# Two sweeps walked backwards with three blocks kept in SBUF, and 1/den and a gradient turned by DMA, in a four-layer forward and backward kernel

## The chip, the cores and the metric

The kernel runs on one core of a Trainium2 chip, as one launch. Its metric is the device time of that launch in microseconds (us). The engines are called by the profile's names: PE is TensorE (its matmuls), PEld TensorE's weight loads, DVE VectorE, ACT ScalarE, POOL GpSimd and SP SyncE, which here only issues DMAs.

## The reference

x has S = 2048 tokens of D = 512. Four layers follow each other, a linear attention A (layers 0 and 2) and a gated layer B with F = 1376 (layers 1 and 3), with the same weights in both pairs:

```python
def A(x, wqkv, wo):                      # H = 32 heads of 16
    q, k, v = heads(x @ wqkv)
    pq, pk = phi(q), phi(k)              # phi(t) = where(t > 0, t + 1, exp(t)) + 1e-6
    kv = einsum("bhsd,bhse->bhde", pk, v)
    z = einsum("bhsd->bhd", pk)
    num = einsum("bhqd,bhde->bhqe", pq, kv)
    den = einsum("bhqd,bhd->bhq", pq, z)[..., None] + 1e-6
    return merge(num / den) @ wo
def B(x, w_gate, w_up, w_down):
    return (sigmoid(x @ w_gate) * (x @ w_up)) @ w_down
x = x + A(layernorm(x));  x = x + B(layernorm(x))      # layers 0 and 1
x = x + A(layernorm(x));  x = x + B(layernorm(x))      # layers 2 and 3
```

The outputs are the last x and the gradients, for a given grad_out, of the input x and of wqkv, wo, w_gate, w_up and w_down. The layernorm has no weights.

## The kernel before, in words

*Tiles and sweeps.* The tokens are cut into 8 blocks of 256 (NBLK, TB). kv and z need every token of a layer before the first q can be used, and the backward pass has the same barrier, so the work is done in five sweeps over the blocks, with a small stage at each barrier, and a last stage for the weight gradients:

- sweep1 (L1492): layernorm of layer 0, k and q of layer 0 (a_k L581, a_q L766), then the barrier (a_barrier L679).
- sweep2 (L1521): the second half of attention layer 0 (a_p2 L796), layer 1 forward (glu_fwd L1188), layernorm and k of layer 2, and its barrier. q of blocks 0 and 1 reuses the turned activations that k used (hTk, kept); for the others h is loaded and turned again (hTq, L773).
- sweep3 (L1550): the second half of attention layer 2 (a_p2), layer 3 forward and backward in one (glu_both L1274), first half of the backward of layer 2 (a_b1 L882), and its barrier (a_bbarrier L983).
- sweep4 (L1589): the second half of the backward of layer 2 (a_b2 L1085), backward of layer 1 (glu_bwd L1383), a_b1 of layer 0, and its barrier.
- sweep5 (L1618): a_b2 of layer 0.
- dw (L1640): weight gradients, the matmuls of L1716, whose operands (dw_set) are loaded and turned by DMA.

All five sweeps take the blocks in the order 0 to 7. What one sweep hands to the next goes through DRAM: x as f32 (xf_d, 512 KB a block, stores SX, loads LX in sweep3), the gradient of x as f32 (dxa_d and dxb_d, 512 KB a block, stores SDX, loads LDX), h, pk, pnT, rphi, dqT and dkT in bf16 (256 KB a block), and layer 1's hh, s2t, and du and dg pairs.

*1/den, in a_p2.* den (DE) is a product of PE with 32 columns of heads per 128 tokens; VectorE adds EPS, takes the reciprocal and writes it as two bf16 parts, high and rest (rr). turn (RT) turns these by two PE transposes (rT_ps). spread (SP) then spreads each head over its 16 rows: four matmuls of 256 columns per block with a matrix of ones and zeros put r_ps in PSUM. VectorE multiplies pq by it (L844, pnT), makes phi' from pq (L847) and multiplies that by r_ps as well (L849, rphiT). pnT is needed by ya_ps (L856), the projection of the attention's output, and pnT and rphi are stored for a_b1.

*The gradient, in a_b1.* ACT casts the gradient of x to bf16 (g), and add_turn (L484) turns it by eight PE transposes a block (L479, gT_ps) and two ACT copies out of PSUM (L481). gT feeds dpn_ps (L914).

*Weights turned for the backward pass.* load_w11T (L1478) loads wdT, wuT and wgT by DMA transposes, the last two in two DMAs each (L1486, L1487). As 1376 is not a multiple of 128, the first rows of the last piece are set to zero by a memset on POOL; load_w11 (L1463) does the same for wd. wgT is then scaled by -0.5 on VectorE.

*What sets the order.* Every step is a piece given to the planner (class Plan, L75): G.add for a step with PE work and the steps of other engines behind it (post, with an engine letter and a duration), G.load and G.store for DMAs. The planner walks through a model of the time before the program is built: a piece may start when its dependencies are met and its buffers (TOKENS, L297: among them 5 PSUM tiles mm, 2 accumulators acc, 20 tiles t2 of 256 KB, 5 tiles xb of 512 KB, 6 tiles s1, 3 pairs pr) are free, and among those that can start on an engine the one with the highest priority goes. The priority is the length of the chain behind a piece, plus a hand-set number from the table OFFSETS (L284). A DMA costs its megabytes by RATE (L87). Each engine executes in the order that comes out. All DMAs are issued on SP's queue, in one order: one whose data is not ready holds those behind it.

The lines of the spread, which the change replaces for six blocks of each attention layer:

```python
for c2 in range(2):
    nc.tensor.matmul(ps[:, c2, :], lhsT=k.spread[:, 2 * hf + c2, :], rhs=st["rT"][:], start=True, stop=True)
yield
sl = slice(2 * hf, 2 * hf + 2)
nc.vector.tensor_tensor(A.pn[b][:, sl, :], pq[:, sl, :], ps[:], ALU.mult)
yield
ph = s1(k, "phq")
nc.vector.tensor_scalar(ph[:], flat(pq[:, sl, :]), -EPS, 1.0, ALU.add, ALU.min)
yield
nc.vector.tensor_tensor(flat(A.rphi[b][:, sl, :]), ph[:], flat(ps[:]), ALU.mult)
```

Of the kernel before, what the change touches and what calls it, by code (L numbers as in the profile page):

```python
# [74 lines left out]
class Plan:  # L75
# [11 lines left out]
    RATE = 0.27  # L87
# [17 lines left out]
    def load(self, key, fn, mb, deps=(), use="", pull=0.0):  # L105
        self.add(key, fn, 0.0, deps, [("D", mb / self.RATE)], use, pull=pull)

# [172 lines left out]
ACCJ, ACCY = 11, 7  # L280
SUMS = {1: ([0, 1], -1), 3: ([2, 3], 1), 5: ([4, 5], 3), 6: ([6], 5), 7: ([7], 6)}
# [3 lines left out]
    CB1:1=-7 DE0:1=-63,2=-19,4=+5,7=+5 DE2:1=-23 DK0:2=+1,4=+21 DP0:0=+36,1=-28,2=+36,3=+36,5=-102 DP2:2=+63,6=-51  # L285
    DT0:+83 DW1:0=-30 DW3:1=+1,7=-2 E3:0=-31,1=+2 G11:0=-7,6=+24,7=+66 G3:1=+1 GS0:3=+31,5=-1,6=-86 GS2:5=+7,6=+44
    J0:1=-74 K0:3=-12 K2:0=+28,1=+28,2=+28,3=+28,4=+29,6=+44,7=+10 LB2:1=-93 LB3:2=-52,3=-12,6=+63,7=+106 LDH0:0=-49
    LDH2:3=+97 LDL0:0=+53,2=+38 LDP0:1=-6 LDP2:3=+41 LDQ0:3=+67 LDX0:0=+113 LDX2:1=-102,2=-13 LG3:0=+7 LH1:6=-75
    LN0:1=-131,5=-68,6=+58 LN2:0=-1 LP0:7=-44 LS1:1=-57 MS0:5=-40 MS2:1=-12,5=-34,7=-87
    Q0:1=-103,2=-115,4=-101,5=-22 Q2:0=-1,1=-23,2=+8 RT0:2=+7 RT2:2=+47 S0:+44 S2:-3 SG2:-64 SH1:2=+17 SN0:4=+50  # L290
    SP0:0=-66 SP2:1=-6,5=-11,7=+1 SPREAD:-24 SQ2:0=+2,6=-77 SU1:3=+1,6=-21 SV1:0=-15,3=+22,6=-13
    TG0:0=+6,1=+3,2=+7,4=+3,5=-18 TG2:6=+38 TK0:2=+113,5=+22,6=+48 TK2:7=+55 TR1:3=-11 UT0:2=-98,3=+2 WGT:-26
    WPL0:+56 WT0:0=-35,1=-40 Y33:7=-97 YA2:5=-43 ZE0:0=+1,3=-2 ZE2:2=+16,4=+19,6=+151 ZS0:5=-8,7=+136 ZS2:7=-52
    ZZ0:+35
# [7 lines left out]
def kernel(  # L302
# [38 lines left out]
    k.rphi_d = {l: dt_(f"rphi_d{l}", [D, S]) for l in (0, 2)}  # L341
# [21 lines left out]
    for l in (0, 2):  # L363
        for nm in ("hT", "pk", "pq", "pn", "rphi", "bh"):
            setattr(k.A[l], nm, {})
# [132 lines left out]
def load_turn(k, key, src, put, name, deps, pull=0.0):  # L498

    def ld():  # L500
        t = t2(k, name)
        put(t)
        k.nc.sync.dma_start_transpose(out=t[:], in_=src)
    k.G.load(f"{key}.0", ld, BLK, deps, "+t2", pull)
    k.G.add(f"{key}.1", lambda: None, 0.0, [f"{key}.0"])


def layernorm(k, l, b, x_fn, deps, sums=False):

    nc, G = k.nc, k.G  # L510

    def half_sums(j):
# [3 lines left out]
        col = slice(2 * b + j, 2 * b + j + 1)  # L516
        rs, sx = k.rstd[l][:, col], k.sx[l][:, col]
# [18 lines left out]
    def half(j):  # L536
# [3 lines left out]
        col = slice(2 * b + j, 2 * b + j + 1)  # L540
# [24 lines left out]
    G.store(f"SH{l}.{b}", lambda: nc.sync.dma_start(out=tok3(k.h_d[l], b), in_=k.h[l, b][:]), BLK, [f"LN{l}.{b}.{j}@h" for j in range(2)])  # L565
# [15 lines left out]
def a_k(k, l, b, keep, by_dma=False):  # L581
# [3 lines left out]
    n = f"{l}.{b}"  # L585

# [9 lines left out]
    if by_dma:  # L596
        load_turn(k, f"TK{n}", k.h_d[l][brows(b), :], put, "hTk", [f"SH{n}"])
    else:
        add_turn(k, f"TK{n}", lambda: k.h[l, b], put, "hTk", [[f"LN{n}.{j}@h"] for j in range(2)])
# [5 lines left out]
    G.store(f"SPK{n}", lambda: nc.sync.dma_start(out=tok3(k.pk_d[l], b), in_=A.pk[b][:]), BLK, [f"K{n}.{j}" for j in range(2)])  # L605
# [160 lines left out]
def a_q(k, l, b, keep, deps):  # L766
    nc, G = k.nc, k.G
    A = k.A[l]
    n = f"{l}.{b}"

    def ld():
        A.hT[b] = t2(k, "hTq")
        nc.sync.dma_start_transpose(out=A.hT[b][:], in_=k.h_d[l][brows(b), :])  # L773

    def half(hf):
# [3 lines left out]
        for c2 in range(2):  # L779
            for m in range(NDC):  # L780
                nc.tensor.matmul(ps[:, c2, :], lhsT=k.wq[:, m, cslice(2 * hf + c2)], rhs=A.hT[b][:, m, :],  # L781
                                 start=(m == 0), stop=(m == NDC - 1))
        yield
        yield from phi(k, flat(A.pq[b][:, 2 * hf:2 * hf + 2, :]), flat(ps[:]))
    if keep:
        src = [f"TK{n}.0", f"TK{n}.1"]
    else:
        G.load(f"LQ{n}", ld, BLK, [f"SH{n}", f"<K{n}.1"] + deps, "+t2")
        src = [f"LQ{n}"]
# [3 lines left out]
    G.free("-t2", [f"<Q{n}.1", f"<K{n}.1"])  # L793


def a_p2(k, l, b, xin_fn, deps, late):  # L796
# [4 lines left out]
    n = f"{l}.{b}"  # L801

# [3 lines left out]
    def den():  # L806
# [9 lines left out]
        yield  # L816
        r = k.p1.tile([P, 2, H], F32, name="rcp", tag="rcp", bufs=2)
# [8 lines left out]
    def turn():  # L826
# [5 lines left out]
        nc.vector.tensor_copy(st["rT"][:], flat(tps[:]))  # L832

# [17 lines left out]
    def y(j):  # L851
# [3 lines left out]
        for c in range(NDC):  # L855
# [4 lines left out]
    G.load("LX" + n, lx, BLK if l == 0 else 2 * BLK, [f"YA{l}.{b - 2}.1", f"SX{l - 1}.{b}"] + deps, "+t2" if l == 0 else "+xb")  # L860
    G.add("DE" + n, den, 8 * 0.027, [f"Q{n}.0", f"Q{n}.1", f"ZZ{l}", f"<YA{l}.{b - 2}.1"],
          [("V", 0.22, "+dn -tp"), ("V", 0.55), ("V", 0.2, "+rr"), ("V", 0.22, "-dn")], "+tp")
    G.add("RT" + n, turn, 2 * C128, ["DE" + n, "SPREAD"] + late, [("V", 0.29, "-tp +rT")], "+tp -rr")
    for hf in range(2):
        G.add(f"SP{n}.{hf}", lambda hf=hf: spread(hf), 2 * C256, ["RT" + n] + ([f"<SP{n}.0"] if hf else []),
              [("V", 0.68, "@pn"), ("V", 0.29, "+s1"), ("V", 0.68, "-s1 -mm")], "+mm" if hf else "+mm +t2 +t2")
    pn = [f"SP{n}.{hf}@pn" for hf in range(2)]
    G.free("-rT", [f"<SP{n}.1"])
    G.free("-t2", [f"SP{n}.0", f"SP{n}.1"])
    G.store(f"SN{n}", lambda: nc.sync.dma_start(out=dmaj(k.pnT_d[l], b), in_=A.pn[b][:]), BLK, pn)  # L870
    G.store(f"SR{n}", lambda: nc.sync.dma_start(out=dmaj(k.rphi_d[l], b), in_=A.rphi[b][:]), BLK, [f"SP{n}.{hf}" for hf in range(2)], "-t2")
# [10 lines left out]
def a_b1(k, l, b, deps):  # L882

    nc, G = k.nc, k.G
# [6 lines left out]
    def ld():  # L891
        A.pn[b] = t2(k, "pnTl")
        nc.sync.dma_start(out=A.pn[b][:], in_=dmaj(k.pnT_d[l], b))
        A.rphi[b] = t2(k, "rphiTl")
        nc.sync.dma_start(out=A.rphi[b][:], in_=dmaj(k.rphi_d[l], b))

    def ldt():
        st["pn"] = t2(k, "pn", [P, 2, D])
        nc.sync.dma_start_transpose(out=st["pn"][:], in_=k.pnT_d[l][:, brows(b)])
# [7 lines left out]
    def dpn(hf):  # L907
# [3 lines left out]
        for c2 in range(2):  # L911
            c = 2 * hf + c2
            for m in range(NDC):
                nc.tensor.matmul(ps[:, c2, :], lhsT=A.WpT[:, m, cslice(c)], rhs=st["gT"][:, m, :],  # L914
# [24 lines left out]
    G.load("LN_" + n, ldt, BLK, [f"SN{n}", f"<MS{l}.{b - 2 if b % 2 else b - 3}.3", f"<DP{l}.{b - 2}.0"] + deps, "+t2")  # L939
# [3 lines left out]
    add_turn(k, f"TG{n}", lambda: st["g"], lambda t: st.__setitem__("gT", t), f"gT{l}", [[f"CA{n}.{j}"] for j in range(2)], pull)  # L943
# [8 lines left out]
    G.store(f"SQ{n}", lambda: nc.sync.dma_start(out=dmaj(k.dqT_d[l], b), in_=st["dq"][:]), BLK, [f"ZE{n}.{hf}" for hf in range(2)], "-t2")  # L952
    if b in MSUMS:
# [26 lines left out]
        G.free(" ".join(["-t2"] * 2 * len(bs)), [f"<MS{n}.3"] + [f"<TG{l}.{bb}.1" for bb in bs])  # L980
# [77 lines left out]
def ln_bwd(k, l, b, j, dh_ps, h, x_in, x_out):  # L1058

    nc = k.nc  # L1060
    rs = (k.rstdh if l in k.rstdh else k.rstd)[l][:, 2 * b + j:2 * b + j + 1]
# [15 lines left out]
def add_lnb(k, l, b, fn, deps, ps_tag, more=""):  # L1077

    for j in range(2):
        k.G.add(f"LB{l}.{b}.{j}", lambda j=j: ln_bwd(k, l, b, j, *fn(j)), 0.0, deps[j] + ([f"LB{l}.{b}.0@s"] if j else []),  # L1080
# [4 lines left out]
def a_b2(k, l, b, x_load, out, deps, out_use=""):  # L1085
# [4 lines left out]
    n = f"{l}.{b}"  # L1090

# [3 lines left out]
    def ldt(nm, src):  # L1095
        st[nm] = t2(k, nm)
        nc.sync.dma_start_transpose(out=st[nm][:], in_=src[brows(b), :])

    def ldq():
        st["dqT"] = t2(k, "dqTl")  # L1100
        nc.sync.dma_start(out=st["dqT"][:], in_=dmaj(k.dqT_d[l], b))

    def ldh():
        st["h"] = t2(k, "hl", [P, 2, D])
        nc.sync.dma_start(out=st["h"][:], in_=tok3(k.h_d[l], b))
# [26 lines left out]
    G.load("LDH" + n, lambda: ldt("hT", k.h_d[l]), BLK, pre, "+t2")  # L1132
    G.load("LDP" + n, lambda: ldt("pkT", k.pk_d[l]), BLK, pre, "+t2")
    G.load("LDQ" + n, ldq, BLK, pre + [f"SQ{n}"], "+t2")
    G.load("LDL" + n, ldh, BLK, pre, "+t2")
    G.load("LDX" + n, ldx, 2 * BLK, pre + [f"SDX{l + 1}.{b}"], "+xb")
# [4 lines left out]
    G.store(f"SK{n}", lambda: nc.sync.dma_start(out=dmaj(k.dkT_d[l], b), in_=st["dkT"][:]), BLK, [f"DK{n}.{hf}" for hf in range(2)])  # L1141
# [3 lines left out]
    add_lnb(k, l, b, lambda j: (st["ps", j][:], st["h"][:, j, :], st["x"][:, j, :], out(st["x"], j)),  # L1145
            [[f"DH{n}.{j}", "LDL" + n, "LDX" + n] for j in range(2)], "mm", out_use)
    G.free("-t2 -t2", [f"<DH{n}.1"])
# [40 lines left out]
def glu_fwd(k, l, b):  # L1188
# [3 lines left out]
    n = f"{l}.{b}"  # L1192
    x = k.x
# [35 lines left out]
    for p in range(NPAIR):  # L1229
# [5 lines left out]
        G.add(f"Y{n}.{p}", lambda p=p: y(p), q * 2 * C512, [f"G{n}.{p}@hh", "WD"] + ([f"<Y{n}.{p - 1}"] if p else []),  # L1235
              [("V", 0.77, "-acc @0"), ("V", 0.77, "-acc")] if p == NPAIR - 1 else [], "" if p else "+acc +acc")
    G.free("-t2", [f"<G{n}.5"])
    G.store("SHH" + n, lambda: store_hh(k, k.hh_d[l], b, st["hh"]), HHB, [f"G{n}.{p}@hh" for p in range(NPAIR)])
    G.store("SS" + n, lambda: nc.sync.dma_start(out=k.s2t_d[b], in_=st["s2t"][:].rearrange("p a c t -> p (a c t)")), 2 * HHB,
            [f"G{n}.{p}" for p in range(NPAIR)], "-w11")  # L1240
    G.store("SX" + n, lambda: nc.sync.dma_start(out=tok3(k.xf_d, b), in_=x[0, b][:]), 2 * BLK, [f"Y{n}.5"])
# [13 lines left out]
def add_dh(k, l, b, st, src):  # L1255
# [8 lines left out]
    for p in range(NPAIR):  # L1264
# [4 lines left out]
        G.store(f"SU{n}.{p}", lambda p=p: store_pair(k, k.du_d[l], b, p, st["pair"][p][0][:]), mb, [f"{src}{n}.{p}@u"])  # L1269
        G.store(f"SV{n}.{p}", lambda p=p: store_pair(k, k.dg_d[l], b, p, st["pair"][p][1][:]), mb, [f"{src}{n}.{p}"])  # L1270
# [3 lines left out]
def glu_both(k, l, b):  # L1274
# [57 lines left out]
    G.load("LG" + n, lg, BLK, [f"<G{l}.{b - 2}.5"] + (["WWD"] if early else [f"<G{l}.{b - 1}.2"]), "+t2")  # L1332
# [18 lines left out]
    add_dh(k, l, b, st, "G")  # L1351
# [482 lines left out]
```

## Time and profile before

| | before |
|---|---|
| median of 3 runs | 1106.6 us (1103.0 to 1108.86) |
| profiled execution | 1106.36 us |
| its span (first to last instruction) | 1104.6 us |
| mean granted clock of TensorE | 0.997 |
| DVE busy | 656.4 us |
| ACT busy | 366.5 us |
| POOL busy | 154.7 us |
| DMA moved | 242.72 MB, mean 220 GB/s |

The profile is one execution, taken by the hardware. In a line of a group of instructions stand the line of the kernel, the engine, the operation, output and inputs by the program's names, the shapes, the number of instructions, then after the bar the busy time in us and the mean duration of one in ns, and after the second bar the idle time of the engine right before them with what ended it. Matmuls overlap, so the mean duration of a matmul is longer than the spacing at which they follow each other. The chain of work that ended last is followed back from the last instruction to what released it. The granted clock is the share of full speed that TensorE's clock had.

### The profile page before, as it was taken

The page shows a single profiled execution, that of the slowest core. Times are in us where ns is not written, and L with a number is a line of the kernel's source. Part 1 is how long each engine was busy: PE and PEld are TensorE (multiplying, and loading weights), DVE is VectorE, ACT ScalarE, POOL GpSimd, SP SyncE. Part 2 cuts the span into 40 slices and gives each one's busy share as a digit, 9 for nine tenths or more (in the row PEclk, how much of TensorE's full clock was granted, in tenths as well). Part 3 has the DMA queues.
Part 4 walks back from the last instruction along what each step waited for, and adds up shares of the span by engine and source line. Part 5 has one row for each costly group of instructions (what it writes and reads, how often), then busy time and mean ns, then how long its engine had stood idle before and what let it go on. Part 6 is the DMA issues. An engine that isn't in the chain of part 4 may idle for free.

```text
span 1104.6 us, 20100 instructions
## 1 busy us (share of the span) xinstructions
PE 1076.5 (97%) x7561; PEld 711.6 (64%) x7660; DVE 656.4 (59%) x1613; ACT 366.5 (33%) x733; POOL 154.7 (14%) x435
## 2 busy tenths in 40 slices
PE   7999999999999999999999999999999999999998
PEld 3667667666666666776665666655554456666787
DVE  6798878588776788767957577767765000000010
ACT  6654555464343334434144434341111000000010
POOL 4135654303122001100000000000000000000000
PEclk9999999999999999999999999999999999999999
DMA  7728996987887767864999899979999999999960
GB/s 237 255 84 263 234 316 200 274 203 193 208 203 197 167 184 202 199 177 127 273 243 274 240 273 264 266 198 253 266 255 267 276 229 205 232 259 223 198 150 20
DMA packets 490338, 242.72 MB, mean 220 GB/s; under 512 B 296224, under 2 KB 474624, under 8 KB 488192
## 3 DMA queue, kind: packets, MB, share of 16 engines
q1 hardware_dynamic: 490240, 241.43, 85.8%
q8 instruction: 60, 0.98, 0.4%
q14 instruction: 38, 0.31, 0.1%
HBM read 68.75 MB, written 100.43 MB: 153 GB/s over the span
## 4 chain that ended last, share of the span: by engine, by line
PE 91%; DMA 4%; DVE 2%; ACT 1%; issue 1%; SPq 1%; ACTq 0%; DVEq 0%
PE dw_ps L1716 24%; PE dha_ps L1129 7%; PE dh_acc L1251 7%; PE dhh_ps L1181 7%; PE g_ps L1181 7%; PE u_ps L1181 7%; PE dh_acc L1249 6%; PE y_ps L1370 3%; PE y_acc L1222 3%; PE dpn_ps L914 2%; PE dpk_ps L1113 2%; PE ya_ps L856 2%; PE k_ps L592 2%; PE m_ps L963 2%; PE q_ps L781 2%; PE g_ps L618 2%
## 5 line engine op out<-in xcount | busy, mean ns | idle before, releaser
L1716 PE MATMUL dw_ps<-dw_set,h 128*128 128x352 bf16 (+2 forms) x1536 | 205.7, 297 | 0.6 <-DMA dw_set<-du_d 0.6
L1716 PEld LDWEIGHTS <-h 128*128 128x128 bf16 x1536 | 150.3, 98 | 56.1 <-issue 0.8
L1698 DVE TENSOR_SCALAR dw_o<-dw_ps 128x512 bf16<-128x512 f32 (+3 forms) x33 | 17.6, 541 | 234.2 <-PE dw_ps L1716 215.5
L1251 PE MATMUL dh_acc<-wgT,dg 128*128 128x512 bf16 x349 | 132.3, 379 | 1.9
L1249 PE MATMUL dh_acc<-wuT,du 128*128 128x512 bf16 x317 | 120.1, 379 | 0.2
L1696 ACT ACTIVATE dw_o<-dw_ps 128x512 bf16<-128x512 f32 (+4 forms) x34 | 16.2, 481 | 246.0 <-PE dw_ps L1716 221.0
L1181 PE MATMUL g_ps<-hT,wg 128*128 128x256 bf16 x704 | 92.5, 273 | 0.1
L1181 PE MATMUL u_ps<-hT,wu 128*128 128x256 bf16 x704 | 92.5, 273 | 0.0
L1181 PE MATMUL dhh_ps<-gT,wdT 128*128 128x256 bf16 x704 | 88.4, 272 | 0.9 <-ACT gT L481 0.7
L1181 PEld LDWEIGHTS <-wg 128*128 128x128 bf16 x704 | 68.1, 98 | 20.5 <-issue 0.4
L1070 POOL TENSOR_SCALAR ab<-c 128x2 f32<-128x2 f32 x64 | 18.6, 291 | 445.1 <-DVE lnb_j L1067 440.2
L1716 PE MATMUL dw_ps<-g,dw_set 128*128 128x512 bf16 (+1 forms) x343 | 77.3, 379 | 2.9 <-DMA dw_set<-hh_d 1.9
L1181 PEld LDWEIGHTS <-wdT 128*128 128x128 bf16 x704 | 68.2, 98 | 12.5 <-issue 1.2
L1181 PEld LDWEIGHTS <-wu 128*128 128x128 bf16 x704 | 68.9, 98 | 8.0
L1716 PEld LDWEIGHTS <-dw_set 128*128 128x128 bf16 (+1 forms) x352 | 35.0, 100 | 41.7 <-DMA dw_set<-hh_d 2.4
L1251 PEld LDWEIGHTS <-dg 128*128 128x128 bf16 x352 | 34.4, 98 | 33.4
L1249 PEld LDWEIGHTS <-du 128*128 128x128 bf16 x352 | 34.4, 98 | 33.4
L1064 ACT ACTIVATE lnb_t<-dha_ps,rstd 128x512 f32<-128x512 f32 x32 | 22.0, 688 | 82.2 <-PE dha_ps L1129 48.5
L481 ACT COPY gT<-gT_ps 128x512 bf16<-128x512 bf16 x48 | 28.2, 588 | 59.8 <-PE gT_ps L479 59.8
L1304 ACT ACTIVATE th<-g_ps 128x512 f32<-128x512 f32 (+1 forms) x48 | 26.8, 558 | 53.7 <-PE g_ps L1181 47.1
L1211 DVE SCALAR_TENSOR_TENSOR hh<-th,u_ps 128x512 bf16<-128x512 f32 (+1 forms) x48 | 30.4, 639 | 19.6 <-ACT th L1206 13.7
L1222 PE MATMUL y_acc<-wd,hh 128*128 128x512 bf16 x165 | 41.5, 379 | 0.6
(201 smaller groups left out, 1846.5 us busy)
## 6 DMA issues: line engine op xcount, KB each, us to landing
s2t_d<-s2t SPq DMA_DIRECT2D x8, 1408.0 KB, 6.5
s2tl<-s2t_d SPq DMA_DIRECT2D x8, 1408.0 KB, 8.4
hh_d<-hh SPq DMA_DIRECT2D x16, 640.0 KB, 4.5
du_d<-du SPq DMA_DIRECT2D x80, 128.0 KB, 2.9
dg_d<-dg SPq DMA_DIRECT2D x80, 128.0 KB, 2.7
h_d<-h SPq DMA_DIRECT2D x32, 256.0 KB, 2.8
h<-h_d SPq DMA_DIRECT2D x18, 256.0 KB, 4.7
pk_d<-pk SPq DMA_DIRECT2D x16, 256.0 KB, 2.7
```

Source lines behind the costliest of these rows:

```text
L481: nc.scalar.copy(dst[:, :, tslice(j)], ps[:])
L592: nc.tensor.matmul(ps[:], lhsT=A.hT[b][:, m, tslice(j)], rhs=k.wk[:, m, :], start=(m == 0), stop=(m == NDC - 1))
L618: nc.tensor.matmul(ps[:], lhsT=k.h[l, bb][:, j, cslice(m)], rhs=A.pk[bb][:, j, :], start=(first and i == 0), stop=(last and i == len(its) ...
L1129: nc.tensor.matmul(ps[:], lhsT=lh[:, c, tslice(j)], rhs=rh[:, c, :], start=(i + c == 0), stop=(i == 2 and c == NDC - 1))
L1181: nc.tensor.matmul(ps[:, i, :], lhsT=w[:, m, fsl(fc)], rhs=rhsT[:, m, :], start=(m == 0), stop=(m == NDC - 1))
L1211: nc.vector.scalar_tensor_tensor(hh, th[:, 0:w], 1.0, flat(up[:])[:, 0:w], ALU.add, ALU.mult)
L1222: nc.tensor.matmul(st["acc"][j][:], lhsT=st["hh"][:, fc, tslice(j)], rhs=k.wd[:, fc, :], start=(fc == 0), stop=(fc == NFC - 1))
L1249: nc.tensor.matmul(acc[j][:], lhsT=du[:, i, tslice(j)], rhs=k.wuT[:, fc, :], start=(fc == 0), stop=False)
L1251: nc.tensor.matmul(acc[j][:], lhsT=dg[:, i, tslice(j)], rhs=k.wgT[:, fc, :], start=False, stop=(fc == NFC - 1))
L1304: nc.scalar.activation(th[:, 0:w], flat(gp[:])[:, 0:w], ACT.Tanh, scale=0.5)
L1370: nc.tensor.matmul(ps[:], lhsT=st["hh"][:, fc, tslice(j)], rhs=k.wd[:, fc, :], start=(fc == 0), stop=(fc == NFC - 1))
L1716: nc.tensor.matmul(ps, lhsT=lhs(s_), rhs=rhs(s_), start=(s_ == 0), stop=(s_ == 31))
```

## The change

*Backwards.* Sweeps 2 and 4 take the blocks from 7 down to 0. In the code b stays the position in the sweep, and B = NBLK - 1 - b (C where the sweep before or after is meant) is the block. The last blocks of one sweep are thereby the first of the next. KEEP and KEEPX: for three blocks at each turn-around (x between sweeps 2 and 3, its gradient between 3 and 4 and between 4 and 5) the f32 tile stays in its xb buffer, and its store and its load are left out; dq of the same blocks stays in SBUF for a_b2 (its store stays, for the weight gradients). KEEPQ: the last two turned blocks hTk of layer 2 are kept for q, as the first two were. In layer 0 all q use the kept hTk, from block 7 down.

*1/den.* For positions 2 to 7 of both attention layers (RDMA), the reciprocal, [128 tokens, 32 heads] in f32, is copied with each head repeated 16 times to a [128, 512] bf16 tile, two per block, by ACT in layer 0 and by POOL in layer 2. A DMA transpose from SBUF to SBUF turns each tile (128 KB) to [128, 4, 128], and VectorE multiplies from there. The two PE transposes, the four spreading matmuls, the split into two bf16 parts and the copy of rT are left out for these blocks. Positions 0 and 1 stay as they were.

*The gradient of layer 2.* For all eight blocks (SBT), g is turned by two such DMA transposes of 128 KB in place of the eight PE transposes and the two ACT copies.

*Smaller parts.* rphi is stored with 2 KB in a row instead of 512 bytes. The memsets of the padding go from POOL to VectorE, as pieces of their own behind the load (add_zero). The planner costs DMA transposes by a rate of their own (TURNED), and OFFSETS is replaced as a whole, which moves pieces against each other in every sweep.

The core of the diff:

```diff
-    RATE = 0.27
+    RATE, TURNED = 0.27, 0.235
...
+KEEP = (3, 3)
+KEEPX, KEEPQ = 3, 2
+RDMA = (2, 2)
+SBT = range(8)
...
 def layernorm(k, l, b, x_fn, deps, sums=False):
+    B = NBLK - 1 - b if l in (1, 2) else b
...
 def a_q(k, l, b, keep, deps):
+    C = NBLK - 1 - b
+    B = b if l else C
+    hT = A.hT if keep else {}
...
-        nc.sync.dma_start_transpose(out=A.hT[b][:], in_=k.h_d[l][brows(b), :])
+        hT[C] = t2(k, "hTq")
+        nc.sync.dma_start_transpose(out=hT[C][:], in_=k.h_d[l][brows(B), :])
...
-def a_p2(k, l, b, xin_fn, deps, late):
+def a_p2(k, l, b, xin_fn, deps, late, by_dma):
...
+        if by_dma:
+            r = k.p1.tile([P, 2, H], F32, name="rcp", tag="rcp", bufs=2)
+            nc.vector.reciprocal(r[:], dn[:])
+            for j in range(2):
+                yield
+                st["rx", j] = s1(k, "rx")
+                src = r[:, j, :].unsqueeze(2).to_broadcast([P, H, D // H])
+                dst = st["rx", j][:].rearrange("p (h e) -> p h e", h=H)
+                if l == 0:
+                    nc.scalar.copy(dst, src)
+                else:
+                    nc.gpsimd.tensor_copy(dst, src)
+            return
...
+    def turn_by_dma(j):
+        if j == 0:
+            st["rT"] = t2(k, "rTx", [P, 2, NDC, P])
+        nc.sync.dma_start_transpose(out=st["rT"][:, j, :, :], in_=st["rx", j][:])
+
+    def spread_turned(hf):
...
+        nc.vector.tensor_tensor(by_tile(A.pn[b]), by_tile(A.pq[b]), rT, ALU.mult)
+        yield
+        rphi = by_tile(A.rphi[b])
+        nc.vector.tensor_scalar(rphi, by_tile(A.pq[b]), -EPS, 1.0, ALU.add, ALU.min)
+        yield
+        nc.vector.tensor_tensor(rphi, rphi, rT, ALU.mult)
...
+    if l and b < KEEPX:
+        G.add("LX" + n, lx, 0.0, [f"LN2.{C}.{j}" for j in range(2)])
+    else:
+        G.load("LX" + n, lx, BLK if l == 0 else 2 * BLK, [f"YA{l}.{b - 2}.1"] + ([f"SX1.{C}"] if l else []) + deps, "+t2" if l == 0 else "+xb")
...
 def a_b1(k, l, b, deps):
+    B = b if l else NBLK - 1 - b
...
+    if l == 2 and b in SBT:
+        def turn(j):
+            if j == 0:
+                st["gTt"] = t2(k, "gT2", [P, 2, NDC, P])
+                st["gT"] = lambda m: st["gTt"][:, :, m, :]
+            nc.sync.dma_start_transpose(out=st["gTt"][:, j, :, :], in_=st["g"][:, j, :])
...
+    kept = b >= NBLK - KEEP[l // 2]
...
+    if kept:
+        A.dq[NBLK - 1 - b] = st
...
 def a_b2(k, l, b, x_load, out, deps, out_use=""):
+    C = NBLK - 1 - b
+    B = C if l else b
+    kept = b < KEEP[l // 2]
...
+    if b < NBLK - KEEPX:
+        G.store("SX" + n, lambda: nc.sync.dma_start(out=tok3(k.xf_d, B), in_=x[0, b][:]), 2 * BLK, [f"Y{n}.5"])
...
+    if b < NBLK - KEEP[1]:
+        G.store(f"SDX{n}", lambda: nc.sync.dma_start(out=tok3(k.dxa_d, b), in_=k.dx[l, b][:]), 2 * BLK, [f"LB{n}.{j}" for j in range(2)])
...
-        nc.gpsimd.memset(t[0:NFC * P - F, NFC - 1, :], 0.0)
...
+def add_zero(k, key, get, dep):
+    k.G.add(key, lambda: k.nc.vector.memset(get()[0:NFC * P - F, NFC - 1, :], 0.0), 0.0, [dep], [("V", 0.3)])
```

## The prediction

> **What bounds the kernel now.** I read the page first (busy time, then the chain), then the chain in order of time, then the stretches in which TensorE stood idle.
>
> ```profile
> PE 1076.5 (97%) x7561; PEld 711.6 (64%) x7660; DVE 656.4 (59%) x1613; ACT 366.5 (33%) x733; POOL 154.7 (14%) x435
> ...
> PE 91%; DMA 4%; DVE 2%; ACT 1%; issue 1%; SPq 1%; ACTq 0%; DVEq 0%
> ```
>
> TensorE is busy 97% of the span and holds 91% of the chain: a matmul taken out shortens the span, and little else does. Three pieces of the chain give the price of one, because matmuls behind each other overlap (start, us, what):
>
> ```profile
> 78.86 0.87 PE u_ps L1181 x8
> ...
> 238.81 0.89 PE kv_ps L696 x16
> ...
> 246.48 3.95 DMA hTq<-h_d
> ```
>
> So 256 columns cost 0.87/8 = 0.109 us and 128 columns 0.89/16 = 0.056 us (512 columns: 0.216 us). The program has 7660 matmuls (2328 of 512 columns, 3520 of 256, 532 of 128, the rest 352, 336 and less). At the spacings of the trace they add up to 1071.7 us. The first starts at 6.9 us and the last at 1101.4 us, so the idle and slow moments in between sum to 22.9 us: about 10 us before 100 us, 5.5 us between 240 and 255, 1.3 us at 541, 2.1 us at 756 and 1.9 us in the last stage.
>
> Two of these places carry a second cost. In the stretches below the columns are stretch, length, busy time and count of PE, PEld, DVE, ACT and POOL, granted clock, DMA share and GB/s:
>
> ```profile
> 58.00:66.00 8.00, 5.43 (x37) 3.36 (x38) 8.00 (x21) 5.34 (x11) 3.31 (x12) 0.96 0.32 98
> 66.00:75.00 9.00, 9.00 (x81) 6.93 (x80) 7.09 (x20) 5.74 (x12) 4.19 (x13) 0.84 0.30 89
> 246.00:250.50 4.50, 1.25 (x7) 0.40 (x6) 3.64 (x9) 0.80 (x3) 1.45 (x3) 0.91 0.87 157
> 250.50:255.00 4.50, 4.50 (x31) 3.57 (x32) 1.79 (x5) 2.07 (x5) 3.01 (x8) 0.71 1.16 246
> ```
>
> After each idle place the clock drops: 0.84 and 0.71 are means over one stretch of 3.4 us at half clock each, so each idle place costs 1.7 us more. In the first, VectorE is full (8.00 of 8.00): it is the bound there. In the second nothing is full. There the queue of SP tells why (start, us):
>
> ```profile
> 237.93 7.15 SPq L1486 DMA_TRANSPOSE wgT<-in_B_w_gate_dram  x1
> 245.13 1.25 SPq L1487 DMA_TRANSPOSE wgT<-in_B_w_gate_dram  x1
> 246.48 1.25 SPq L773 DMA_TRANSPOSE hTq<-h_d  x1
> ```
>
> The load that PE waited for (3.4 us) was issued only when the two turns of wgT had left SP's queue.
>
> **The change, part by part.**
>
> *Matmuls removed.* By the built programs' order: 24 turns of 1/den (12 blocks x 2, 128 columns), 48 spreading matmuls (12 x 4, 256 columns), 64 turns of the gradient (8 blocks x 8, 128 columns). 24 x 0.056 + 48 x 0.109 + 64 x 0.056 = 1.3 + 5.2 + 3.6 = 10.2 us, all on the path. Nothing is added on PE (7524 matmuls remain).
>
> *What takes their place.* Per block of 1/den: two copies of 128x512 and two DMA turns out of SBUF; then VectorE's products read SBUF instead of PSUM.
>
> ```profile
> L844 DVE TENSOR_TENSOR pnT<-pqT,r_ps 128x512 bf16<-128x512 bf16 x32 | 21.1, 683 | 8.9 <-PE r_ps L841 8.8
> L1424 DVE TENSOR_TENSOR dg<-s2tl,dhh 128x512 bf16<-128x512 bf16 x40 | 16.7, 419 | 1.5 <-DMA dg_d<-dg 1.5
> ...
> L847 DVE TENSOR_SCALAR phq<-pqT 128x512 bf16<-128x512 bf16 x32 | 8.7, 293 | 0.0
> ```
>
> A product of the same shape out of SBUF takes 0.42 us, not 0.68. Per block VectorE loses 2 x (0.68 + 0.29 + 0.68) + 0.73 (rr and rT) = 4.0 us and gains 2 x (0.42 + 0.29 + 0.42) = 2.3 us: 12 x 1.7 = 20 us less, beside PE's work, so nothing on the path. The copies go to ACT in layer 0 and to POOL in layer 2. Nearest rows: an ACT copy of this shape 0.59 us, POOL's s2t at L1213 0.66 us; 12 each, on engines busy 33% and 14%. The 64 turns of the gradient also had 16 ACT copies of 0.59 us; they go.
>
> *The DMA turns: 40 of 128 KB, from SBUF.* No row of before turns out of SBUF. Nearest: turns of 256 KB out of DRAM, 1.25 us on SP's queue and 4.0 us to landing. Lower bound: half of it, 0.6 us of queue. Upper bound: 5 us, the longest issue of pn (L899), when the DMA engines were backed up. I take 1.25 us and 4.0 us, the row itself. The Trainium skill speaks against this part: "VectorE: DVE Perf Modes", section "The three transpose paths", gives 390 ns for a 128x128 turn on TensorE and 1309 ns by DMA. By that rule 64 gradient turns would trade 25 us for 84 us. By the trace they trade 64 x 0.056 = 3.6 us of the full engine for 16 x 1.25 = 20 us of a queue that waits much of the time between 258 and 535 us (DMA share 0.73). The rule counts one turn alone; here only the throughput of PE counts, so I take the trace.
>
> Does the wait show? A block of 1/den needs, from den to pn: 0.2 (PE) + 0.8 (VectorE) + 1.3 (two copies) + 1.25 + 4.0 (second turn) + 0.8 (pn) = 8.4 us. The new order leaves 9 us of PE work between them for block 2 of each layer (9.1 in layer 0) and 10 us or more for the others: hidden, with 0.7 us to spare at the tightest. If it is late, VectorE stands at pn, with the evacuations of the GLU behind it, and PE's buffers fill. The gradient's last block is tighter: before, from the last dh_acc (517.1 us) to both halves of g cast (523.6 us) took 6.5 us; with a second issue and landing (about 4.7 us) that is 11.2 us, against 10.4 us of PE work that the new order puts in between. With VectorE's usual lateness I charge 1.5 us.
>
> *Walking backwards, three blocks kept.* 18 transfers of 512 KB and 6 of 256 KB disappear (10.5 MB of 241 MB); 5 MB of turns are added. These loads were hidden: no idle place of PE above names them. Worth nothing by itself. Pieces of rphi grow to 2 KB: also off the path.
>
> *The order at the second turn-around (225 to 255 us).* SP's new order is wuT, seven plain transfers, hTq, wgT, two stores, hTq. wuT stands right behind wdT, so SP is through with it near 221 us and the first hTq goes at about 228 us, as soon as its block's k is stored. wgT follows until about 236.5 us; the second hTq lands near 241.5 us. PE reaches it after 231.4 us of its own work plus some 10 us of accumulated idle: 241.4 us. The wait shrinks from 3.4 to about 0.5 us. The half clock goes too: the Trainium skill, "TensorE: Matmul & The Clock Gate", section "What's actually happening", says that an idle window of about 3.4 us drops the clock to half for at least one more. The trace agrees at 249.7 us, but at 65.4 us it dropped after several waits of 0.3 to 1.3 us within 4 us, so by the rule both drops would go, by the trace only the second. Together 3.4 - 0.5 + 1.7 = 4.6; I take 4.0, since the other waits there stay.
>
> *The first turn-around (45 to 75 us).* VectorE bounds it. Adding up its instructions at their measured durations: 56.2 us of work before pn of block 1 in the old order, 61.6 us in the new (all q's now come first), while PE has 3 us more work in front of that place. The two nearly cancel. The memsets of the padding move from POOL, which stood 15.4, 14.7 and 9.7 us for them with the layernorm's steps queued behind, to VectorE: 3 x 0.3 us, and a wait of 0 to 1.5 us for wd, which landed at 55.9 us. Net I take -0.5 us.
>
> **Sum**, from the profiled execution (1106.36 us, span 1104.6, 1.8 around it; the median of the runs shown is 1106.6): 1106.4 - 10.2 - 4.0 - 0.5 + 1.5 = 1093.2, so 1093 us.
>
> **Rivals.**
> *The idle places close further.* 22.9 us of idle are there to win, and the new order is a new layout of all of them. For it: VectorE has 20 us less to do, the transfers at the starts of the fourth and fifth stage go, where PE waited 2.1 us at 756. Against it: most of those places wait for VectorE or for dw_set, which stay. Another 6 us: 1087 us.
> *The turns are late.* If a turn out of SBUF takes 8 us instead of 4, block 2 is 3.3 us late, the last gradient about 5.5 us in all, and one more drop of the clock costs 1.7 us: +9, 1102 us.
> *Slower: SP's queue fills up.* Place: 258 to 535 us, where some 26 of the turns go. Adding up the issue times there, SP is in use some 155 of 277 us; 26 turns fit in the free 122 us while each takes less than 4.7 us. From there on the stores of du and dg come late, the three pair buffers stay taken and PE waits. At 6 us each: 26 x 1.3 = 34 us more, 1127 us. Against it: only one of 16 pn issues was that long.
> *The blocks kept do nothing:* already assumed.
>
> **How the numbers follow.** 1093 us 0.55 (own range 1089 to 1098), 1087 us 0.20, 1102 us 0.20, 1127 us 0.05. A measurement here tells 0.5% (5.5 us) from no change. Faster (under 1101): 0.55 + 0.20 + 0.11 = 0.86; within: 0.09; slower: 0.05. The range from 1084 to 1104 leaves out the slow rival and the tails.
>
> **What would show it.** Right: rT_ps and r_ps down to 4 blocks' worth, gT_ps to 64 matmuls fewer, PE's busy sum lower by about 10 us; no half clock near 240 us; turns out of SBUF of about 1.25 us on SP. Wrong: PE waiting for VectorE's pn or for gT2, turns of more than 3 us, a drop of the clock at a new place, or idle at 60 us larger than now.

## The result, and the profile after

The changed kernel takes 1094.2 us (median of 4 runs, 1092.7 to 1095.0) where the kernel before took 1104.8 us (4 runs, 1102.9 to 1108.9): a ratio of 0.990, interval 0.986 to 0.993. The prediction was 1093 us, its range 1084 to 1104. Its profiled execution took 1094.62 us with a span of 1092.9 us. Between the medians the fall is 10.6 us, and between the two profiles (1106.36 us before) 11.7 us.

The same lines of the page as before, busy time by engine and the chain by engine:

```profile
PE 1069.8 (98%) x7524; PEld 700.9 (64%) x7524; DVE 640.5 (59%) x1580; ACT 363.5 (33%) x729; POOL 171.6 (16%) x444
...
PE 72%; DVE 2%; DMA 1%; SPq 1%; issue 1%; ACT 0%; POOL 0%; DVEq 0%; ACTq 0%; POOLq 0%
```

The shares of this chain don't add up to 100, so I don't read its 72% as less work on PE. I add up instead, as in the prediction: the 7524 matmuls at the spacings of their trace are 1061.8 us (before 1071.7), the first starts at 6.9 and the last at 1089.7 us, so 21.0 us are idle or slow clock (before 22.9). The difference of 11.7 us in span is 9.9 us of matmuls and 1.8 us of idle. These sums are good to some 0.3 us: the spacing of the 512 matmuls of 336 columns reads 142 or 143 ns from trace to trace, and with one set of spacings for both kernels it is 10.2 and 1.6 us. Cut by place, from the same matmul starts (a half clock counts as idle for the time it costs):

| us of idle on PE | before | after | after, second profile |
|---|---|---|---|
| first turn-around (25 to 75 us) | 6.0 | 5.3 | 5.3 |
| second turn-around (225 to 275) | 5.4 | 2.0 | 2.0 |
| third sweep (275 to 500) | 0.4 | 1.7 | 3.5 |
| its end, third turn-around (500 to 575) | 1.9 | 2.3 | 2.3 |
| last turn-around (700 to 775) | 3.0 | 5.6 | 3.7 |
| last stage (775 on) | 1.8 | 0.1 | 1.4 |
| all, with the start | 22.9 | 21.0 | 22.0 |

The stretches that were shown of before (length, busy time and count by engine, granted clock, DMA share, GB/s), with the one ahead of the second turn-around's, which now begins earlier:

```profile
58.00:66.00 8.00, 7.42 (x73) 5.27 (x70) 7.88 (x24) 4.99 (x11) 0.83 (x4) 1.00 0.12 45
66.00:75.00 9.00, 6.52 (x62) 4.83 (x62) 8.23 (x23) 8.49 (x19) 6.06 (x19) 1.00 0.51 150
...
238.00:246.00 8.00, 7.50 (x69) 5.90 (x67) 8.00 (x20) 3.71 (x7) 0.00 (x0) 1.00 0.47 117
246.00:250.50 4.50, 4.50 (x51) 4.06 (x50) 3.83 (x12) 4.29 (x10) 3.26 (x12) 1.00 0.00 0
250.50:255.00 4.50, 3.87 (x37) 2.90 (x35) 3.48 (x9) 3.48 (x7) 1.24 (x3) 1.00 0.32 66
```

Both half clocks are gone (0.84 and 0.71 before, 1.00 in all five rows); a new one came at 735 us, in this profile only of the two (last section). VectorE is full at both turn-arounds now (7.88 of 8.00 and 8.23 of 9.00; 8.00 of 8.00). On SP's queue the loads stand as forecast (start, us):

```profile
223.54 1.29 SPq L782 DMA_TRANSPOSE hTq<-h_d  x1
224.93 5.65 SPq L1573 DMA_TRANSPOSE wgT<-in_B_w_gate_dram  x1
...
233.61 1.68 SPq L782 DMA_TRANSPOSE hTq<-h_d  x1
```

The first hTq went at 223.5 us where the forecast had 228, the second at 233.6 us; no matmul waited for either.

The new instructions, from the groups by tile (min, median and max in ns):

```profile
L861 SPq DMA_TRANSPOSE rTx<-rx x24: 1188/1220/2516, 67.7 to 421.7; - x24
L872 DVE TENSOR_TENSOR pnT<-pqT,rTx x24: 405/418/828, 73.1 to 427.6; 128x512 bf16<-128x512 bf16 x24
...
DMA to landing us min/median/max: 2.4/2.6/5.5
```

```profile
L837 ACT CAST rx<-rcp x12: 601/606/618, 66.1 to 147.2; 128x512 bf16<-128x512 f32 x12
L839 POOL CAST rx<-rcp x12: 609/613/1075, 250.4 to 419.2; 128x512 bf16<-128x512 f32 x12
```

A turn of 128 KB out of SBUF holds SP 1.22 us (1.25 estimated) and lands after 2.6 us (4.0 estimated); the copies (0.61 us) and the product (0.42 us) are as estimated.

### The profile page after: what moved, and what is told of

It is laid out like the page before. It is cut to its first block, busy times and chain, and to the rows that moved or that the text cites. A ratio compares the mean times of both kernels' runs of the same rounds, so it can differ in the third digit from the quotient of the medians.

```text
span 1092.9 us, 19982 instructions
## 1 busy us (share of the span) xinstructions
PE 1069.8 (98%) x7524; PEld 700.9 (64%) x7524; DVE 640.5 (59%) x1580; ACT 363.5 (33%) x729; POOL 171.6 (16%) x444
## 4 chain that ended last, share of the span: by engine, by line
PE 72%; DVE 2%; DMA 1%; SPq 1%; issue 1%; ACT 0%; POOL 0%; DVEq 0%; ACTq 0%; POOLq 0%
PE dw_ps L1818 26%; PE dha_ps L1205 8%; PE dh_acc L1336 6%; PE dh_acc L1334 6%; PE dhh_ps L1264 6%; PE y_ps L1456 3%; PE g_ps L1264 3%; PE u_ps L1264 3%; PE dpk_ps L1189 3%; PE m_ps L1036 2%; PE dpn_ps L975 2%; PE ya_ps L901 1%; DMA dw_set<-hh_d 1%; DMA rTx<-rx 1%; PE gT_ps L483 1%; PE dpn_ps L988 1%
## 5 line engine op out<-in xcount | busy, mean ns | idle before, releaser
L1334 PE MATMUL dh_acc<-wuT,du 128*128 128x512 bf16 x352 | 133.4, 379 | 0.0
L1818 PE MATMUL dw_ps<-g,dw_set 128*128 128x512 bf16 (+1 forms) x352 | 79.5, 384 | 3.8 <-DMA dw_set<-hh_d 3.8
L1509 DVE TENSOR_TENSOR du<-s2tl,dhh 128x512 bf16<-128x512 bf16 (+1 forms) x48 | 18.9, 400 | 41.3 <-ACT dhh L1504 35.7
```

What stands on the lines that cost most here:

```text
L1334: nc.tensor.matmul(acc[j][:], lhsT=du[:, i, tslice(j)], rhs=k.wuT[:, fc, :], start=(fc == 0), stop=False)
L1818: nc.tensor.matmul(ps, lhsT=lhs(s_), rhs=rhs(s_), start=(s_ == 0), stop=(s_ == 31))
```

## The experiments

Each was timed beside the kernel before on the same chip; the chips differ a little, so ratios are compared. "Idle" is worked out as above, from one profile. For some kernels the profiled run lies above the median of their runs: memset_back by 4.7 us, no_keep by 3.0, before_wgt_late by 1.7. The changed kernel was run again beside three of them:

> The changed kernel itself, beside the next three on their chip: the ratio of before, 0.990 within 0.003, and idle places as in its first profile.

The ratio came as expected, 0.990. The idle places did not all: the third sweep had 3.5 us instead of 1.7, and the last turn-around 3.7 instead of 5.6 (second profile, in the table above).

| kernel | ratio to before, interval | matmuls, us | idle, us |
|---|---|---|---|
| changed, again | 0.990 (0.988 to 0.992) | 1061.8 | 22.0 |
| work_back | 0.998 (0.996 to 0.999) | 1072.0 | 21.1 |
| no_turns | 1.011 (1.010 to 1.013) | 1072.0 | 36.5 |
| turns_only | 1.013 (1.010 to 1.016) | 1061.6 | 49.0 |
| no_keep | 1.005 (1.003 to 1.006) | 1061.8 | 41.2 |
| dead_traffic | 1.007 (1.004 to 1.009) | 1061.8 | 40.9 |
| dead_spread | 0.997 (0.995 to 0.998) | 1061.6 | 26.6 |
| turns_plus | 1.028 (1.026 to 1.030) | 1061.6 | 61.6 |
| memset_back | 0.994 (0.992 to 0.995) | 1061.6 | 29.5 |
| before_wgt_late | 1.010 (1.008 to 1.012) | 1072.0 | 37.2 |
| before_wgt_dve | 1.006 (1.004 to 1.009) | 1071.7 | 27.0 |
| s0_early | 0.995 (0.993 to 0.997) | 1061.8 | 27.1 |

My theory: the gain is the matmuls, on the path in any order, plus the second turn-around; the kept blocks are worth nothing. The rival: the gain is the order and the transfers saved.

**work_back: the matmuls alone, in the same order.**

```python
if by_dma and j == 0:
    for n in (128, 128, 256, 256, 256, 256):
        nc.tensor.matmul(ps[:, 0:n], lhsT=A.pn[b][:, 0, tslice(j)], rhs=A.Wp[:, 0, 0:n], start=True, stop=True)
...
if l == 2 and hf == 0:
    for m in 2 * list(range(NDC)):
        nc.tensor.matmul(ps[:, 0, 0:P], lhsT=A.WpT[:, m, cslice(0)], rhs=st["gTt"][:, 0, m, :], start=True, stop=True)
```

> The changed kernel with 136 idle matmuls put back near the places of those that the change removed (24 of 128 columns and 48 of 256 ahead of ya_ps, 64 of 128 ahead of dpn_ps; their results are written over), in the same order of everything else. If every matmul is on the path: PE's sum up by 10.2 us and the time too, about 1104.5 us, idle on PE as before. If the change's gain lay in its order and its transfers, and the matmuls could be hidden in the 21 us of idle that are left: up by 5 us or less, below 1100 us, with the idle places smaller.

The page's first lines:

```profile
span 1103.3 us, 20248 instructions
...
PE 1080.4 (98%) x7660; PEld 710.8 (64%) x7660; DVE 640.6 (58%) x1580; ACT 363.7 (33%) x729; POOL 171.8 (16%) x444
```

The span is 10.4 us above 1092.9, and 9.5 above that of the second profile (1093.8); the matmuls' sum is 10.2 us higher and the idle the same (21.1 against 21.0). The 136 matmuls are worth their spacing, to within a microsecond; the idle places didn't take any of it. By the ratios, which are coarser, they are worth 0.008 (0.990 to 0.998), about 9 us. What work_back still gains on the kernel before, 0.002 (1 to 4 us), is all that the rest of the change (order, kept blocks, smaller parts, with the turns on SP's queue) is worth together.

**The parts alone.** no_turns sets `RDMA = (8, 8)` and `SBT = ()`. turns_only puts the same turns by DMA into the kernel before (positions 2 to 7 of 1/den, layer 2's gradient), with its order table and the walk forward.

> The changed kernel with all blocks of 1/den and of the gradient turned by PE again; blocks are still kept and walked backwards. The planner orders anew. If the turns are the change's gain: PE's sum up by 10 us, about 1104 to 1107 us. If the order and the blocks kept are the gain: below 1098 us.

> The kernel before, walked forward and with nothing kept, with only the turns of 1/den (blocks 2 to 7 of both layers) and of layer 2's gradient moved to DMA; the planner orders anew with the old table. If the removed matmuls are worth their 10 us in any order and the forward walk has no need of kept blocks: PE's sum down by 10 us and the idle within 5 us of before's, 0.987 to 0.995 of before. If the turns need the new order to be hidden: idle up by 8 us or more, 0.998 of before or worse.

The matmul sums moved by 10 us as expected in both, but the idle did not stay: 36.5 and 49.0 us. Of the 49.0 us of turns_only, 13.1 are at the second turn-around (5.4 before) and 15.1 at the third (1.9 before). What PE waited for, from the waits (us in total, times, longest):

```profile
PE dhh_ps L1238 <- DMA gT<-in_grad_out_dram: 5.6, 2, 4.2
PE dpk_ps L1170 <- DMA hT<-h_d: 3.1, 1, 3.1
PE gT_ps L481 <- ACT g L1466: 2.9, 1, 2.9
PE k_ps L594 <- DMA hTk<-h_d: 2.2, 2, 1.3
```

These are mostly transfers that were in time before, but the turns by DMA are not what holds the longest of them. The gT of 4.2 us was issued at 252.6 us behind the two turns of wgT (245.0 to 252.5 us), where none of the new turns stands. The hT of 3.1 us was issued at 545.3 us (528.3 us before): the planner had put it behind the last gradient's two turns (540.4 to 543.1 us) and behind the store of MT, whose data came at 544.9 us. So turns_only shows that the turns do not pay in the order that the planner made with the old table, not that they need the walk backwards or the kept blocks. Both kernels mix their part with an order table that was fitted to another kernel, so the 24 and 26 us by which their ratios stand above the changed kernel's are not the price of a part.

**no_keep, dead_traffic and dead_spread: what the kept blocks are worth.** no_keep sets `KEEP = (0, 0)` and `KEEPX, KEEPQ = 0, 0`, and the planner orders anew. The other two keep the blocks and the order, and only put dead copies of the saved volume on SP's queue: dead_traffic where the loads would stand, dead_spread behind the stores of hh and the loads of s2t:

```python
k.nc.sync.dma_start(out=k.dead_d[o:o + rows, :].rearrange("(n p) d -> p n d", p=P),
                    in_=k.g_in[0:rows, :].rearrange("(n p) d -> p n d", p=P))
```

> The changed kernel with no block kept in SBUF: the 18 transfers of 512 KB and 6 of 256 KB are back, hTq of all eight blocks of layer 2 is loaded, the turns by DMA and the walk backwards stay. If those transfers were hidden: 1094 us within 3 us, the more so where the new wait would be at the second turn-around, at most 3 us for hTq. If the saved 10.5 MB were part of the gain, at 0.22 MB per us 48 us of transfers come back and an eighth of it showing would be 6 us: 1100 us or more.

> The changed kernel in its own order, with the transfers that the kept blocks save put back as dead ones: at each of the nine kept blocks two copies of 512 KB from one DRAM place to another, and one of 256 KB at the six of dq, on SP's queue where the loads would stand. Nothing waits for them. If no_keep lost its 18 us because data of the kept blocks had to make the way out and back before use: within 3 us of the changed kernel. If it lost them to the traffic and to SP's queue: 1104 us or more, with the stops at the three turn-arounds as in no_keep (7.6, 5.5 and 5.3 us longer than in the changed kernel).

> The changed kernel in its own order, with dead copies of the same volume as the saved transfers (21 of 512 KB, from DRAM to DRAM) spread over the second, third and fourth sweep, behind each block's stores of hh and behind the loads of s2t, so away from the turn-arounds. If dead_traffic lost its 19 us by its place (ahead of the gradient's second turn and of hTq): within 4 us of the changed kernel. If the volume itself costs: 8 us or more, with stops in the middle of the sweeps.

The idle of no_keep grew by 7.6 us at the second turn-around (9.6 against 2.0), 5.6 at the third and 6.2 at the last. dead_traffic, in which nobody waits for the copies, lost nearly as much. Its worst place, from the chain in order of time:

```profile
521.12 0.55 SPq L1020
521.73 0.59 SPq L809
522.37 0.62 SPq L809
523.04 0.64 SPq L809
523.78 6.51 DMA gT<-g
```

Three dead copies (L809) came between the two turns of the last gradient; the second went 2 us later and took 6.5 us to land instead of 2.6, and PE waited 5.2 us. Away from the turn-arounds the same volume costs less but not nothing: dead_spread is 0.007 slower than the changed kernel, about 7.6 us, between my two expectations. Its profile has 4.6 to 5.6 us more idle, nearly all in the third sweep (7.5 against 1.7 and 3.5 us), where again a turn was late. My theory falls here: in the changed kernel the kept blocks are worth something. At the place shown it is a turn that the copies hold up, so the turns use room that the kept blocks leave on the queue. How much of the loss goes that way is not shown: no run has the new order with the transfers and without the turns, and the dead copies run from DRAM to DRAM, which the saved transfers did not.

**turns_plus: how much room SP's queue has.** Four more turns behind each second turn of the third sweep, in the same order:

```python
for i in range(4):
    k.again_i = (k.again_i + 1) % 8
    t = k.hs if k.again_i < 4 else k.spread
    k.nc.sync.dma_start_transpose(out=t[:, k.again_i % 4, :], in_=src)
```

> The changed kernel in its own order, with four more turns (128x128, into places no longer used) behind each second turn out of SBUF of the third sweep: 56 turns, at 1.2 us each 67 us more of SP's queue between 258 and 530 us, where by the issue times some 90 us are free. If the queue has that room: within 4 us of the changed kernel. If the slower rival's filling begins earlier than its sum said, because free time lies between waits: 8 us or more, with PE waiting for buffers of du and dg or for loads behind the turns.

The queue where the extra turns (hs, spread) follow those of block 2 (start, us), then the waits of the third sweep:

```profile
279.50 2.50 SPq L868 DMA_TRANSPOSE rTx<-rx  x2
282.05 4.08 SPq L492 DMA_TRANSPOSE spread<-rx  x3
286.18 1.23 SPq L492 DMA_TRANSPOSE hs<-rx  x1
287.51 0.53 SPq L1475 DMA_DIRECT2D out_dram<-o  x1
288.08 2.55 SPq L868 DMA_TRANSPOSE rTx<-rx  x2
```

```profile
DVE pnT L881 <- DMA rTx<-rx: 11.7, 3, 5.0
PEld L797 <- DMA hTq<-h_d: 10.4, 3, 4.5
DVE x2l L912 <- DMA x2l<-xf_d: 10.1, 1, 10.1
```

By issue times SP was in use for 152 of 277 us in the third sweep before, 185 of 270 us in the changed kernel, and 254 of 305 us here; and 40 us of idle came with it, not less than 4. By that sum the extra turns still fitted into the 270 us, but issues in a row also lie 0.075 us apart, and with these gaps it is 274 us. So this run just overfills the queue, and does not tell how far below full the loss begins. That some of it begins earlier is shown by the changed kernel itself, with 185 of 270 us in use (next section).

**The second turn-around: before_wgt_late, before_wgt_dve, memset_back.** before_wgt_late adds `WGT0:-120` to the order table of the kernel before; before_wgt_dve also puts the memsets of wuT and wgT on VectorE as in the change (add_zero). memset_back takes the changed kernel in its order and issues the three memsets on POOL again, with the loads.

> The kernel before with one number added to the order's table, so that both turns of wgT are issued behind the first loads of hTq instead of ahead of them. If the second turn-around's idle place (5.4 us between 225 and 275 us) was that queue's doing: the wait for hTq down to 0.5 us and the half clock gone, 3.5 to 4.5 us less on PE there, 0.996 of before. If wgT's own lateness takes its place at dh_acc: no gain, 1.000 of before.

The first expectation failed: hTq did come in time (1.3 us of waits), but PE stood 7.7 us at dhh_ps. What held it, from POOL's timeline:

```profile
253.46 0.51 POOL L1488 MEMSET wgT<- 32x512 bf16 x1 [17.26 <-DMA wgT<-in_B_w_gate_dram]
253.95 0.18 POOL L521 TENSOR_TENSOR ln_q<-sx,pm 128x2 f32<-128x2 f32 x1
254.21 1.47 POOL L523 TENSOR_SCALAR ln_q<-ln_q 128x1 f32<-128x1 f32 x1
```

POOL stood 17.3 us at the memset until wgT had landed; the layernorm's steps (L521 on) were behind it, ACT behind those, and the evacuation of dhh_ps behind ACT.

> The kernel before with wgT behind the loads of hTq, as in before_wgt_late (12.9 us of idle and half clock between 225 and 275 us), and with the memsets of wuT and wgT as steps of their own on VectorE. If POOL's wait was what cost there: the stop of 7.7 us at dhh_ps and the half clock go, 2 to 4 us are left between 225 and 275 us (5.4 in the kernel before), and the time falls by 9 us from before_wgt_late, to about 1110 us. If wgT itself was late: 10 us or more stay there.

The stop of 7.7 us and the half clock went: 5.7 us are left there instead of 12.9, where I had expected 2 to 4. By the ratios the time fell by 0.004, about 4 us, and not by 9. And 5.7 us is no better than the 5.4 us of the kernel before: most of the waits that are left are for VectorE (2.0 us for rphiT, 1.2 us for pqT; 0.5 us for hTq). So in the old order the DMA's wait is replaced by VectorE's. The changed kernel has 2.0 us there; which of its moves does that was not taken apart.

> The changed kernel in its own order, with only the zeroing of the padding of wd, wuT and wgT back on POOL, issued with the loads as in the kernel before. In the kernel with wgT issued late, PE stood 7.7 us because POOL waited with that memset for wgT to land and the layernorm's steps were queued behind it. If the memsets' move is a part of the gain: the same kind of stop comes back between 228 and 262 us, 4 to 10 us in all. If it is worth the 0.5 us that the prediction gave it: 1094 to 1097 us, idle places as in the changed kernel.

The ratio is 0.004 worse, about 4.6 us, which has the size of the first expectation, but not at its place: between 225 and 275 us nothing came back (some 2 us of idle, as in the changed kernel). What did come is at another memset. POOL's timeline:

```profile
214.54 0.52 POOL L1576 MEMSET wuT<- 32x512 bf16 x1 [5.19 <-DMA wuT<-in_B_w_up_dram]
215.15 0.19 POOL L528 TENSOR_SCALAR ln_q<-ln_q 128x1 f32<-128x1 f32 x1
```

2.3 us of new idle stand right behind it, at 216 and 220 us (hTk_ps waits for ACT, ACT for POOL's ln_q). The rest of that profile's extra idle is in the third sweep (7.5 us), at a place that varies from one execution to the next (the turn of 1/den at 356 us, next section); whether the memsets have a part in it stays open.

**s0_early.** `S0:-40` in the order table becomes `S0:+33`.

> The changed kernel with one number of the order's table changed, so that the first dw_set load is issued ahead of the turns of hT and pkT for the fifth sweep instead of behind them (some 4.3 us earlier). If PE's stop of 3.9 us at 731 us is this load's lateness and the half clock after it (1.7 us) its follower: both go, 5.6 us less, about 1089 us. If another load, such as hT, pkT or pn, is then late in its place: 1092 to 1095 us, with the stop at another line.

The chain there:

```profile
732.75 1.73 PE dw_ps L1818 x8
734.48 0.10 PE gT_ps L483 x2
734.59 8.08 DMA dw_set<-hh_d
```

The matmuls of the first dw_set began 2 us earlier, but they last 1.7 us, and the second dw_set, pushed behind hT, pn and pkT, landed at 742.7 us: PE's stop is 5.3 us instead of 3.9, and two steps of half clock begin in it instead of one behind it. The second expectation had the mechanism, another load that is late in its place, but at most 1 us of loss; the ratio of 0.995 is about 6 us.

## Why the prediction was right

*Matmuls removed, -10.2 us:* right, in size and in mechanism. The traces give -9.9 to -10.2, and work_back +10.2 with the idle unchanged.

*VectorE, 20 us less, nothing on the path:* 15.9 us less by the page. The count fits (36 fewer, 3 memsets more), and so do the new rows (0.45, 0.28 and 0.41 us); the missing 4 us are spread over its other instructions, which I did not trace further.

*The turns out of SBUF, 1.25 and 4.0 us:* 1.22 and 2.6 us. Both kinds of turn are alike (gT<-g: median 1.21 and 2.6 us). The nearest row of the trace was the better guide than the Trainium skill's 1309 ns ("VectorE: DVE Perf Modes", section "The three transpose paths") counted for each 128x128.

*1/den hidden, with 0.7 us to spare at the tightest:* nearly. Block 2 of layer 2 shows (start, us, what):

```profile
280.54 1.22 SPq L861
...
282.44 1.22 SPq L861
283.71 3.63 DMA rTx<-rx
...
287.44 0.76 DVE pnT L872 x2
...
289.61 0.61 DVE hh L1398
290.21 0.04 issue
290.26 0.81 PE ya_ps L901 x3
```

Three turns and a store stood in a row on SP. pn itself was just in time: the first four ya_ps began at 288.2 us, as it was done. But VectorE had stood at it, with an evacuation of the GLU (hh) behind it, and the next ya_ps waited for that: 1.2 us of idle. This is the way that the prediction gave for a late turn. At 356 us a turn of 1/den stands behind one of gT (2.5 us), and VectorE stands 2.5 us until it lands; in the second profile PE lost 1.3 us behind it, and 0.6 us more at 428 us. I had 0 for this and measured 1.2 and 3.0 us. The rival "the turns are late" named the place; the turns themselves are not slow, the queue in front of them is.

*The last gradient of the third sweep, +1.5 us:* 0.4 us. The turn landed in 2.6 us.

*Second turn-around, -4.0 us:* -3.5 us, and the half clock is gone. The queue's order came as read. But before_wgt_dve shows that this order alone does not give it: VectorE's waits would have taken the place.

*First turn-around, -0.5 us:* -0.7 us, but by luck. The waits themselves grew, from 4.3 to 5.3 us. What went is the half clock (1.7 us), for which the sum had nothing, and the old order does not have it in every execution: before_wgt_late, in which every engine has the order of the kernel before up to 230 us, had no half clock there and 4.1 us of idle, 1.2 us less than the changed kernel. What the new order does is spread the waits: at most 1.9 us of them fall into any stretch of 3.41 us, where the old order has up to 2.5 us (2.2 us in before_wgt_late). None of the ten profiles of the changed kernel and its variants shows a half clock there; the last section tells why it comes and goes.

*The memsets:* nothing in the sum ahead of the second turn-around; memset_back shows 2.3 us there. In the old order with wgT late the same memsets cost 7.7 us, and I had looked at them only at the first turn-around.

*Blocks kept, "worth nothing by itself":* wrong as stated. The transfers were hidden before; but put back into the changed kernel, with its 40 turns, the same volume cost 5 to 8 us spread out and 19 us at the turn-arounds.

*The slower rival, SP's queue:* its chance was low and it did not come; but its point was set too far off. I had let turns fit up to 4.7 us each, since the free time of the sum was 122 us. With 69 us more of turns, which makes 3.7 us of queue for each of the 28 of that sweep, PE lost 40 us. Part of it is the sum, which had left out the gaps between issues (11 us before).

*What no step had:* the last turn-around is 0.7 to 2.6 us worse. The first dw_set is issued behind two turns and lands 3.7 to 3.9 us late, and in the first profile a half clock follows, a drop at a new place, which the prediction had named as a sign of being wrong:

```profile
726.56 8.19 DMA dw_set<-hh_d
734.75 0.05 issue
734.79 3.43 PE dw_ps L1818 x8
```

The last stage is 0.4 to 1.7 us better. These two about cancel, so the sum's -3.0 us of idle met -1.8 and -0.9 us. The total was close because its large term was certain; of the small ones, some met by luck. Counted from the profile the forecast fall was 13.2 us; the profiles give 11.7 and the medians 10.6.

## What to carry to other kernels

On a kernel that PE bounds, price removed matmuls at their spacing; with the order held, work_back gave just that. Idle is a property of the order: every experiment that let the planner order anew, one number of its table included, cost 4 to 26 us of idle, so a part's worth is only measured with the order held (work put back, dead transfers). And a queue's room is not all of its free time: when work is moved to a queue that is in use two thirds of the time, look for what stands behind each new entry, and what else leaves that queue.

## What the runs showed of the hardware

*A turn costs SP the same at a quarter of the size.* The 128x128 turns of turns_plus took 1.23 us (median) and landed in 2.3 us, those of 128x512 1.22 and 2.6 us.

*The half clock comes in steps of 3.41 us, and what counts is how much of one step PE stood idle.* At the last turn-around the same kernel stood 3.92 us in one execution and 3.72 us in another. The stretches behind the stop, first of the one and then of the other (the number right after the last count is the granted clock):

```profile
734.70:740.00 5.30, 5.21 (x24) 2.62 (x25) 1.36 (x7) 1.09 (x2) 0.00 (x0) 0.68 1.05 203
```

```profile
736.00:741.00 5.00, 4.85 (x33) 2.87 (x34) 2.73 (x13) 1.10 (x2) 0.00 (x0) 1.00 1.19 202
```

Only the first lost 1.7 us more. In other runs a stop of 3.13 us at this place (no_turns) was followed by half clock and one of 3.50 us (dead_spread) was not. Within each trace the half-clock stretches last 3.41 us or a multiple and start on one grid of that step. The Trainium skill, "TensorE: Matmul & The Clock Gate", section "What's actually happening", says that the window runs freely; that fits.

The grid, laid over the matmul starts, tells more. Nine of the traces have a record of every matmul. In them, PE stood idle 2.18 us or more in 17 of the steps at full clock, and half clock followed every time. Of the other steps, nearly 2800, one was followed by half clock (2.10 us idle); the highest without it have 2.11 and 2.09 us. So the limit in these traces is about 2.1 us of idle in one step of 3.41 us, in one wait or in several. The stop of 3.92 us put 3.20 us into one step; that of 3.72 us fell on two, with 2.11 and 1.62 us. At the first turn-around of the kernel before, several short waits made 2.30 us in one step; in before_wgt_late, with the same order there, no step has more than 1.2 us, as the grid falls elsewhere. The prediction spoke of an idle window: here a step that was idle for six tenths was enough.

This is a part of what makes executions differ. In the profiles a granted clock of 1.000 goes with no such step ahead of the last matmul, 0.998 with one, 0.997 with two, 0.995 with three. By this count the 59 executions of the kernel before that were timed beside the experiments had 1.5 steps on average (5 had none, 25 had one, 22 had two), and the ten of the changed kernel 1.1. So on average the change saved under one half clock, not the two that went from the rows shown of before: what went at the first two turn-arounds came back in good part at the last.
